# Banded attention and two FFNs on one core: the first FFN's eighth pair of weight chunks converted inline, and a smaller early allowance for the planner

## The chip, the core and the metric

The kernel runs on one core of a Trainium2 chip. The metric is the device time of one execution in microseconds. The core has five engines that run their own instruction streams in order: PE (TensorE, matmuls, with a separate row PEld for weight loads), DVE (VectorE), ACT (ScalarE), POOL (GpSimd) and SP (SyncE, which here only issues DMAs). They wait for one another through semaphores.

## The reference

```
attention: q, k, v of 4 x 8 heads x 576 tokens x 64
  scores = q k^T / 8, masked: heads 0-3 the last 32 keys, heads 4-7 every 4th of the last 128
  softmax over the keys, times v  ->  x: 2304 tokens x 512
first FFN:  h = x @ w_in (512 x 2048);  g = h if h > 0 else exp(h) - 1;  y = g @ w_out (2048 x 512)
second FFN: out = ((y @ w_a) * (y @ w_b)) @ w_out2        (512 x 1536, twice, then 1536 x 512)
```

The weights come to the chip as 64-bit floats. The kernel makes two 32-bit halves of each (a high part and a remainder), and each matrix product of the FFNs is three passes on TensorE: high x high, high x low, low x high.

## The kernel before

**Steps of the first FFN.** The tokens are cut in six blocks of 384 (t = 0 to 5), the 2048 hidden columns in 16 chunks of 128 (f = 0 to 15). One step s is one pair (t, f) of `STEPS1`: 7 steps of block 0, then all 16 of block 1 (steps 7 to 22), the remaining 9 of block 0 (23 to 31), then blocks 2 to 5, 96 steps in all. In a step PE does 12 matmuls into `ps_h` (line 525, "h(s)" below); ACT makes relu and exp of it into the tile `el` (lines 546 and 547), DVE joins them with line 552 ("el(s)" below), ACT and POOL split the result into the halves of `g` (lines 536 and 537), and two steps later PE does the 12 matmuls of the second product into four banks of `ps_y` (line 571, "y(s)" below). PE's order is h(s), y(s-2), h(s+1), y(s-1), and so on. There are two `ps_h` banks, so h(s+2) can start only when el(s) is done. When a block of tokens is complete its four `ps_y` banks are copied out, two by ACT (line 608) and two by DVE (line 606); for the first part of block 0 that is in step 8, and y(7) needs the same four banks again.

**Attention inside the steps.** Attention of block t+1 or so runs between the matmuls: scores (line 474), mask and maximum on DVE (490, 356), exp on ACT (360), normalisation on POOL (370), transposes (499) with ACT copies (502), values (514), and the split of x on ACT and DVE (462, 463). These tiles share two `ps_a` banks. For block 2 it starts at step 18, for block 3 at step 29.

**Weight conversion.** One chunk of w_in or w_out is 128 x 512 doubles. Converting it takes three ACT instructions (high word 252, low word 257, copy of the high part 278) and four on DVE (clamp 262, join 267, sign 270, remainder 297 or 854). Chunk f of w_out ("1o", f) and chunk f+2 of w_in ("1i", f+2) form a pair. There are two ways of doing it:

- inline: lines 1401 to 1404 put the two loads in step f-1 and the whole conversion (`w_convert`) in step f; the converted tile lies in the pool `pw`, named "w", which has 16 buffers, all used by the pairs f = 0 to 6 and the first two chunks;
- by the planner: `chunk_ops` splits the conversion into single operations, and `tick`, called twice a step from step 7 on (lines 1461 to 1464), places as many of them as the allowance of each engine admits. The allowance grows by `ROOM1` per tick in the first 32 ticks (steps 7 to 22) and by `ROOM` after that, and is spent by the costs in `COST` (0.7 for a 512-wide DVE operation, 0.67 on ACT). The converted tile lies in the pool "wb", which is opened in step 6. After the chunks of the first FFN the same list goes on with the weights of the second FFN (lines 901 and 917 are its DVE operations), whose results go to DRAM and come back later.

Both kinds share four buffers for raw weights (`wraw`) and four for the work tile (`wt`).

Of the kernel before, what the change touches and what calls it, by code (L numbers as in the profile page):

```python
# [36 lines left out]
SPLIT = 7  # L37
# [16 lines left out]
C1, C0, AHEAD, LAG_IN, LAG_OUT = SPLIT, NF1 + SPLIT, 56, 3, 2  # L54
LATE, LAG_LATE = 2 * (NF1 * (NB - 1) - C1), 7

ROOM1 = {"V": 1.8, "A": 1.4, "G": 0.9}
ROOM = {"V": 1.15, "A": 0.95, "G": 0.75}

FILL = [1, 1, 0, 1, 2, 1, 0] + [1, 1, 0, 1, 2, 0, 0]  # L60
# [2 lines left out]
ON0, ON1 = "AAV", "AAV"  # L63
# [152 lines left out]
def banded_attention_two_ffn(ctx: ExitStack, tc: tile.TileContext, ins, out):  # L216
    nc = tc.nc
    V, A, G, T, SP = nc.vector, nc.scalar, nc.gpsimd, nc.tensor, nc.sync
# [577 lines left out]
    def tick(behind_exp=False):  # L796
        now[0] += 1
        size = ROOM1 if now[0] <= 2 * (C0 - C1) else ROOM
        for e in room:
# [43 lines left out]
    def chunk_ops(key):  # L843

        at = {}
        x = assembly(at)(key)

        def hi():
            at["to"] = pools["wb"].tile([128, 2, 512], F32R, tag="w", name="w")
            part_hi("A", at["to"][:, 0, :], at["t", key])  # L850

        def lo():
            w = w_sb[key] = at["to"]
            V.tensor_tensor(w[:, 1, :], at["t", key], f32(w[:, 0, :]), op=SUB)

        give("wraw", x)
        give("wt", Op("V", 512, lo, Op("A", 512, hi, x)))
# [464 lines left out]
    def at_step(step, slot, fn, *args):  # L1322
        todo.setdefault((step, slot), []).append((fn, args))
# [70 lines left out]
    for f in range(NF1):  # L1394
        st = f
        ks = [("1o", f)] + ([("1i", f + 2)] if f + 2 < NF1 else [])
        if f >= SPLIT:
            for k in ks[::-1]:
                chunk_ops(k)
            continue  # L1400
        for k in ks:
            if k != ("1o", 0):
                at_step(max(0, st - 1), "B" if f else "L", w_load, k)
        at_step(st, "C", w_convert, ks, "w", ON1)


    def held(fn, *args):
# [170 lines left out]
```

## Time and profile before

| | us |
|---|---|
| median of 3 runs (lowest, highest) | 916.47 (914.46, 916.89) |
| the profiled execution | 915.85 |
| its span | 914.0 |
| PE busy in the span | 897.7 (98%) |
| DVE busy | 657.5 (72%) |
| ACT busy | 522.7 (57%) |
| POOL busy | 284.1 (31%) |

The span begins with the first instruction and ends with the last; the 1.85 us around it belong to the execution's time. The busy shares are means over very different stages: PE's row of tenths in the page reads 9 nearly everywhere, DVE's is between 8 and 9 in the first fifth and 5 to 7 after that.

### The profile page before, as it was taken

What the parts mean: (1) busy time and instruction counts of PE and PEld (TensorE: products, weight loads), DVE (VectorE), ACT (ScalarE), POOL (GpSimd) and SP (SyncE); (2) the same over time, 40 slices, a digit from 0 to 9 for tenths busy, and PEclk for the clock granted to TensorE, in tenths of its full rate; (3) what the DMA queues carried; (4) which work ended last, traced back from release to release, by engine and by line L of the source; (5) the groups of instructions that cost most, each with busy time, mean ns of one, the idle gap of its engine ahead of it and who ended that gap; (6) DMA issues with size and microseconds to landing.
All of it is one profiled execution on the core that took longest, in us unless ns stands there. A gap on an engine that the chain in (4) does not pass through costs nothing.

```text
span 914.0 us, 17034 instructions
## 1 busy us (share of the span) xinstructions
PE 897.7 (98%) x6157; PEld 862.7 (94%) x6157; DVE 657.5 (72%) x1147; ACT 522.7 (57%) x1328; POOL 284.1 (31%) x260
## 2 busy tenths in 40 slices
PE   9999999999999999999999999999999999999998
PEld 6789988899999999999999999999999999999998
DVE  6898899759767777767876366688746688656666
ACT  6898788777777777876766343325443225343231
POOL 2323234333333333332323122222622222522233
PEclk9999999999999999999999999999999999999999
DMA  9764344648656455645997588675787754687722
GB/s 286 227 225 164 134 150 144 219 144 271 198 178 217 157 176 192 207 160 184 327 356 270 179 289 281 226 259 179 233 329 252 252 196 144 226 311 242 243 69 70
DMA packets 75860, 195.80 MB, mean 214 GB/s; under 512 B 8288, under 2 KB 22240, under 8 KB 75776
## 3 DMA queue, kind: packets, MB, share of 16 engines
q1 hardware_dynamic: 63680, 175.70, 57.0%
q10 hardware_dynamic: 12096, 19.01, 5.7%
q8 instruction: 49, 0.80, 0.3%
q14 instruction: 35, 0.29, 0.1%
HBM read 151.16 MB, written 43.52 MB: 213 GB/s over the span
## 4 chain that ended last, share of the span: by engine, by line
PE 72%; DVE 4%; issue 1%; ACT 0%; DVEq 0%
PE ps_h L974 27%; PE ps_y L571 14%; PE ps_h L525 14%; PE ps_o L1290 13%; PE ps_s L474 1%; PE ps_v L514 1%; PE ps_o L1150 1%; PE ps_t L499 1%; DVE u L1082 0%; DVE yt L733 0%; DVE acc L1313 0%; DVE u L1064 0%; DVE y L703 0%; DVE wraw L917 0%; DVE u L1046 0%
## 5 line engine op out<-in xcount | busy, mean ns | idle before, releaser
L974 PE MATMUL ps_h<-y,w 128*128 128x384 f32 x1512 | 293.0, 337 | 1.5 <-DVE el L1029 1.1
L974 PEld LDWEIGHTS ps_h<-y,w 128*128 128x128 f32 x1512 | 256.0, 188 | 4.4 <-DVE el L1029 2.0
L571 PE MATMUL ps_y<-g,w 128*128 128x384 f32 x1152 | 224.4, 341 | 2.0 <-ACT w L278 1.4
L525 PE MATMUL ps_h<-x,w 128*128 128x384 f32 x1152 | 222.9, 340 | 3.6 <-DVE el L552 2.1
L525 PEld LDWEIGHTS ps_h<-x,w 128*128 128x128 f32 x1152 | 199.0, 188 | 9.0 <-DVE el L552 3.2
L571 PEld LDWEIGHTS ps_y<-g,w 128*128 128x128 f32 x1152 | 200.4, 189 | 6.3 <-ACT w L278 1.8
L537 POOL TENSOR_TENSOR g<-el,g 128x384 fp32r<-128x384 f32 x96 | 116.6, 1215 | 276.7 <-ACT g L536 230.7
L1290 PE MATMUL ps_o<-w,g 128*128 128x256 f32 x1071 | 153.4, 281 | 0.4 <-ACT g L1090 0.4
L1290 PEld LDWEIGHTS ps_o<-w,g 128*128 128x128 f32 x1071 | 147.2, 188 | 0.9 <-ACT g L1090 0.9
L552 DVE SCALAR_TENSOR_TENSOR el<-el,ps_h 128x384 f32<-128x384 f32 x96 | 53.0, 552 | 80.4 <-ACT el L547 78.0
L1016 POOL TENSOR_TENSOR g<-el,g 128x384 fp32r<-128x384 f32 x34 | 38.4, 1131 | 121.7 <-ACT g L1015 106.8
L1313 DVE TENSOR_TENSOR acc<-acc,ps_o 128x512 f32<-128x512 f32 (+1 forms) x77 | 49.7, 645 | 34.3 <-PE ps_o L1290 34.0
L546 ACT ACTIVATE el<-ps_h 128x384 f32<-128x384 f32 x96 | 46.5, 485 | 38.4 <-PE ps_h L525 33.6
L267 DVE SCALAR_TENSOR_TENSOR wt<-wt,wraw 128x512 uint32<-128x512 uint32 x68 | 62.2, 919 | 3.8 <-ACT wraw L257 1.4
L270 DVE SCALAR_TENSOR_TENSOR wt<-wraw,wt 128x512 uint32<-128x512 uint32 x68 | 60.5, 895 | 0.8
L536 ACT ACTIVATE g<-el 128x384 fp32r<-128x384 f32 x96 | 49.6, 516 | 16.7 <-DVE el L552 16.6
L370 POOL TENSOR_TENSOR e<-e,rs 96x512 f32<-96x512 f32 (+2 forms) x40 | 40.7, 1018 | 47.1 <-DVE rs L369 47.1
L547 ACT ACTIVATE el<-el 128x384 f32<-128x384 f32 x96 | 50.2, 523 | 1.7
L360 ACT ACTIVATE e<-e,nm 96x128 f32<-96x128 f32 x128 | 49.8, 391 | 0.7
L257 ACT ACTIVATE wraw<-wraw 128x512 uint32<-128x512 uint32 x68 | 45.1, 669 | 5.4 <-DMA wraw<-in_w2o 2.8
L1064 DVE TENSOR_TENSOR u<-ps_h,u 128x384 f32<-128x384 f32 x36 | 20.0, 557 | 39.0 <-PE ps_h L974 39.0
L1025 ACT COPY el<-ps_h 128x384 f32<-128x384 f32 x36 | 17.2, 478 | 50.4 <-PE ps_h L974 50.4
(111 smaller groups left out, 1084.0 us busy)
## 6 DMA issues: line engine op xcount, KB each, us to landing
w<-w2P_o SPq DMA_DIRECT2D x52, 512.0 KB, 5.6
w<-w2P_a SPq DMA_DIRECT2D x48, 512.0 KB, 4.5
w<-w2P_b SPq DMA_DIRECT2D x48, 512.0 KB, 4.4
wraw<-in_w1i SPq DMA_DIRECT2D x16, 512.0 KB, 4.1
wraw<-in_w1o SPq DMA_DIRECT2D x16, 512.0 KB, 3.5
wraw<-in_w2a SPq DMA_DIRECT2D x12, 512.0 KB, 3.6
wraw<-in_w2b SPq DMA_DIRECT2D x12, 512.0 KB, 3.6
wraw<-in_w2o SPq DMA_DIRECT2D x12, 512.0 KB, 3.8
```

Source lines behind the costliest of these rows:

```text
L267: V.scalar_tensor_tensor(t, t, 3, L, op0=ALU.logical_shift_left, op1=ALU.bitwise_or)
L270: V.scalar_tensor_tensor(t, H, 0x80000000, t, op0=ALU.bitwise_and, op1=ALU.bitwise_or)
L360: A.activation(e[:, i], sc[:, i], AF.Exp, bias=nm[:, i : i + 1], scale=scale, accum_out=sm[:, i : i + 1],)
L525: T.matmul(ps[:, :TB], w[:, wi, kc * 128 : (kc + 1) * 128], xs[kc][:, xi, :], start=(n == 0), stop=(n == 3 * KC - 1),)
L536: A.activation(g[:, 0, :], gf, AF.Copy)
L537: G.tensor_tensor(g[:, 1, :], gf, f32(g[:, 0, :]), op=ALU.subtract)
L547: last_e[0] = A.activation(e, e, AF.Exp, scale=-1.0)
L552: last_g[0] = V.scalar_tensor_tensor(e, e, -1.0, h_ps.pop(s)[:, :TB], op0=ALU.add, op1=ALU.max)
L571: T.matmul(y_ps[t][c][:, :TB], w[:, wi, c * 128 : (c + 1) * 128], g[:, gi, :], start=(first and n == 0), stop=(last and n == 2),)
L974: last_mm[0] = T.matmul(ps[:, :TB], w[:, wi, kc * 128 : (kc + 1) * 128], y2[S, yop][kc][:, xi, :], start=(start and n == 0), stop=(n == 5) ...
L1290: T.matmul(ps[:, 256 * n : 256 * n + 256], g[name][:, gi, i * 128 : (i + 1) * 128], w[:, wi, h, :], start=((first or not held) and n == m ...
L1313: V.tensor_tensor(a, a, ps[:, :n], op=ADD)
```

## The change

The pair f = 7 (chunk 7 of w_out and chunk 9 of w_in) is converted inline in step 7 instead of by the planner, into buffers of "wb". The planner is left with 14 chunks of the first FFN instead of 16, and its allowance per tick in steps 7 to 22 goes from 1.8 to 1.5 on DVE and from 1.4 to 1.2 on ACT.

```diff
-ROOM1 = {"V": 1.8, "A": 1.4, "G": 0.9}
+ROOM1 = {"V": 1.5, "A": 1.2, "G": 0.9}
 ...
     for f in range(NF1):
         st = f
         ks = [("1o", f)] + ([("1i", f + 2)] if f + 2 < NF1 else [])
-        if f >= SPLIT:
+        if f > SPLIT:
             for k in ks[::-1]:
                 chunk_ops(k)
             continue
         for k in ks:
             if k != ("1o", 0):
                 at_step(max(0, st - 1), "B" if f else "L", w_load, k)
-        at_step(st, "C", w_convert, ks, "w", ON1)
+        at_step(st, "C", w_convert, ks, "w" if f < SPLIT else "wb", ON1)
```

The loads of the new pair stand in SP's queue where the planner's first two loads stood; the planner's loads begin two places later. What moves on the engines is shown at three places. The first is DVE's stream in steps 6 to 9; lines 262, 267, 270 and 297 are conversion, 552 is el, 606 the copies out of `ps_y`. Before:

```order
125 L463 TENSOR_TENSOR x<-ps_v,x 128x4x96
126 L297 TENSOR_TENSOR w<-wt,w 128x512 x2
127 L552 SCALAR_TENSOR_TENSOR el<-el,ps_h 128x384
128 L606 COPY el<-ps_y 128x384
129 L552 SCALAR_TENSOR_TENSOR el<-el,ps_h 128x384
130 L606 COPY el<-ps_y 128x384
131 L552 SCALAR_TENSOR_TENSOR el<-el,ps_h 128x384
132 L262 TENSOR_SCALAR wt<-wt 128x512
```

And in the changed kernel:

```order
126 L297 TENSOR_TENSOR w<-wt,w 128x512
127 L262 TENSOR_SCALAR wt<-wt 128x512
128 L297 TENSOR_TENSOR w<-wt,w 128x512
129 L262 TENSOR_SCALAR wt<-wt 128x512
130 L267 SCALAR_TENSOR_TENSOR wt<-wt,wraw 128x512
131 L552 SCALAR_TENSOR_TENSOR el<-el,ps_h 128x384
132 L267 SCALAR_TENSOR_TENSOR wt<-wt,wraw 128x512
133 L270 SCALAR_TENSOR_TENSOR wt<-wraw,wt 128x512 x2
134 L552 SCALAR_TENSOR_TENSOR el<-el,ps_h 128x384
135 L297 TENSOR_TENSOR w<-wt,w 128x512 x2
136 L606 COPY el<-ps_y 128x384 x2
137 L552 SCALAR_TENSOR_TENSOR el<-el,ps_h 128x384
```

Eight conversion instructions came in around el(7) and el(8), and both copies of line 606 now stand behind the last two of them. On PE, y(7) is split there in the changed kernel: 3 matmuls, then 7 of h(10), then its other 9.

The second place is DVE's stream between el(16) and el(17), as an example of the steps that the planner fills; 854 is the planner's remainder. Before:

```order
175 L552 SCALAR_TENSOR_TENSOR el<-el,ps_h 128x384
176 L854 TENSOR_TENSOR w<-wt,w 128x512
177 L270 SCALAR_TENSOR_TENSOR wt<-wraw,wt 128x512
178 L262 TENSOR_SCALAR wt<-wt 128x512
179 L267 SCALAR_TENSOR_TENSOR wt<-wt,wraw 128x512
180 L270 SCALAR_TENSOR_TENSOR wt<-wraw,wt 128x512
181 L552 SCALAR_TENSOR_TENSOR el<-el,ps_h 128x384
```

In the changed kernel:

```order
175 L552 SCALAR_TENSOR_TENSOR el<-el,ps_h 128x384
176 L262 TENSOR_SCALAR wt<-wt 128x512
177 L854 TENSOR_TENSOR w<-wt,w 128x512
178 L267 SCALAR_TENSOR_TENSOR wt<-wt,wraw 128x512
179 L270 SCALAR_TENSOR_TENSOR wt<-wraw,wt 128x512
180 L552 SCALAR_TENSOR_TENSOR el<-el,ps_h 128x384
```

Four conversion instructions stand in the step instead of five. Counted in the two streams from the start of the kernel, the conversion instructions on DVE are 64 before and 72 now through step 8, 95 and 98 through step 14, 111 in both through step 17, 149 and 144 through step 25, 159 in both through step 29; from step 30 on the changed kernel is four to nine behind, and behind the last el of the first FFN stand 11 instead of 5.

The third place is ACT's stream in steps 10 and 11; 546 and 547 are relu and exp, 536 the high half of g, the others conversion. Before:

```order
138 L536 ACTIVATE g<-el 128x384
139 L278 ACTIVATE w<-wt 128x512
140 L257 ACTIVATE wraw<-wraw 128x512
141 L546 ACTIVATE el<-ps_h 128x384
142 L278 ACTIVATE w<-wt 128x512
143 L547 ACTIVATE el<-el 128x384
144 L257 ACTIVATE wraw<-wraw 128x512
145 L252 ACTIVATE wt<-wraw 128x512
```

In the changed kernel:

```order
142 L536 ACTIVATE g<-el 128x384
143 L252 ACTIVATE wt<-wraw 128x512
144 L546 ACTIVATE el<-ps_h 128x384
145 L547 ACTIVATE el<-el 128x384
146 L278 ACTIVATE w<-wt 128x512
147 L252 ACTIVATE wt<-wraw 128x512
```

The copy 278, which waits for DVE's line 270, stood between relu and exp of step 11 and now stands behind the exp.

## Rows read from the trace of the kernel before

**Rows 1.** Busy time by stretch: each engine's us (instructions), then PEclk, DMA share, GB/s.
```profile
78.48:109.69 31.21, 31.21 (x181) 31.21 (x181) 24.49 (x39) 24.45 (x50) 8.54 (x8) 1.00 0.44 149
109.69:168.87 59.18, 53.51 (x326) 49.27 (x325) 52.60 (x88) 46.20 (x126) 20.27 (x16) 0.97 0.48 164
162.00:166.00 4.00, 4.00 (x22) 3.72 (x23) 3.05 (x6) 1.42 (x4) 0.00 (x0) 0.57 1.03 331
...
240.00:420.00 180.00, 180.00 (x1242) 172.57 (x1241) 132.60 (x234) 137.83 (x396) 61.46 (x55) 1.00 0.54 181
...
505.00:545.00 40.00, 40.00 (x247) 39.35 (x247) 18.88 (x33) 15.65 (x33) 7.83 (x8) 1.00 0.74 237
```

**Rows 2.** What PE waited for, 112 to 170 us: total, times, longest.
```profile
PE ps_h L525 <- DVE el L552: 2.1, 4, 1.1
PE ps_s L474 <- DVE x L463: 1.6, 1, 1.6
PE ps_v L514 <- ACT pt L502: 1.4, 1, 1.4
PE ps_y L571 <- POOL g L537: 0.4, 1, 0.4
```

**Rows 3.** PE in order of time: start us, us, line, count, [idle before, releaser].
```profile
86.81 2.24 PE L571 MATMUL ps_y<-g,w 128*128 128x384 f32 x12
...
107.61 2.25 PE L571 MATMUL ps_y<-g,w 128*128 128x384 f32 x12
109.69 2.25 PE L525 MATMUL ps_h<-x,w 128*128 128x384 f32 x12
...
135.05 2.35 PE L525 MATMUL ps_h<-x,w 128*128 128x384 f32 x12 [1.06 <-DVE el L552]
...
163.52 3.43 PE L571 MATMUL ps_y<-g,w 128*128 128x384 f32 x12
...
168.87 2.24 PE L571 MATMUL ps_y<-g,w 128*128 128x384 f32 x12
...
173.72 0.68 PE L571 MATMUL ps_y<-g,w 128*128 128x384 f32 x3
174.34 1.12 PE L474 MATMUL ps_s<-qk 64*96 64x128 f32 x16
...
177.15 0.88 PE L514 MATMUL ps_v<-pt,v 128*64 128x96 f32 x16
...
182.23 0.83 PE L499 MATMUL ps_t<-ident,e 96*128 96x96 f32 x8
...
306.50 0.49 PE L499 MATMUL ps_t<-ident,e 96*128 96x96 f32 x4
```

**Rows 4.** DVE in order of time.
```profile
79.29 0.55 DVE L552 SCALAR_TENSOR_TENSOR el<-el,ps_h 128x384 f32<-128x384 f32 x1 [0.66 <-ACT el L547]
79.80 0.56 DVE L606 COPY el<-ps_y 128x384 f32<-128x384 f32 x1
...
85.34 0.69 DVE L267 SCALAR_TENSOR_TENSOR wt<-wt,wraw 128x512 uint32<-128x512 uint32 x1
...
86.89 1.51 DVE L267 SCALAR_TENSOR_TENSOR wt<-wt,wraw 128x512 uint32<-128x512 uint32 x1
...
89.04 0.55 DVE L552 SCALAR_TENSOR_TENSOR el<-el,ps_h 128x384 f32<-128x384 f32 x1
...
113.81 0.55 DVE L552 SCALAR_TENSOR_TENSOR el<-el,ps_h 128x384 f32<-128x384 f32 x1 [1.33 <-ACT el L547]
...
308.12 0.55 DVE L552 SCALAR_TENSOR_TENSOR el<-el,ps_h 128x384 f32<-128x384 f32 x1 [0.53 <-ACT el L547]
```

**Rows 5.** ACT in order of time.
```profile
76.12 0.63 ACT L278 ACTIVATE w<-wt 128x512 fp32r<-128x512 f32 x1 [2.36 <-DVE wt L270]
...
98.15 0.63 ACT L278 ACTIVATE w<-wt 128x512 fp32r<-128x512 f32 x1 [1.99 <-DVE wt L270]
...
165.61 0.69 ACT L257 ACTIVATE wraw<-wraw 128x512 uint32<-128x512 uint32 x1 [2.55 <-DMA wraw<-in_w2o]
```

**Rows 6.** POOL in order of time.
```profile
86.39 1.46 POOL L537 TENSOR_TENSOR g<-el,g 128x384 fp32r<-128x384 f32 x1 [3.27 <-ACT g L536]
```

## The prediction

> **What bounds the kernel now.** I read the page first: PE is busy 98% of the span, so only the places where PE waits, or runs slowly after a wait, can give time back. The view of busy time by stretch shows where those lie. In the 180 us from 240 to 420 PE is busy for all 180, and in the 31.21 us from 78.48 to 109.69 for all 31.21; in the 59.18 us from 109.69 to 168.87 it is busy 53.51, at a mean granted clock of 0.97 [rows 1]. The view of waits says for what: el four times (2.1 us), x of line 463 (1.6), the copy pt of line 502 (1.4), g (0.4) [rows 2]. The reader is to see that all of these are made on DVE and ACT. In that stretch DVE is busy 52.60 of 59.18 us, in the one before only 24.49 of 31.21 [rows 1].
>
> The timeline shows how it comes to that. el(s) may end as late as 3 groups of 12 matmuls after h(s), since h(s+2) starts there. A group takes 2.08 us: ten of them lie between the starts at 86.81 and 107.61 [rows 3]. So the limit is 6.24 us. h(10) ends at 86.81 and el(10) starts at 89.04, 2.23 us later; h(15) ends at 107.61 and el(15) starts at 113.81, 6.20 later [rows 3, 4]. In five steps the planner's five DVE instructions a step have used up the whole reserve, with ACT and DVE waiting for each other on the way: line 278 waited 1.99 us for line 270 at 98.15 and held up the exp behind it [rows 5]. All that attention adds from step 18 on then falls on PE.
>
> **What that stretch loses.** From 109.69 to 168.87 the timeline has 21 groups, three sets of scores, one of transposes and one of values. The 21 groups are 43.7 us. A set of scores inside y costs 3.43 (173.72 to 177.15) less 2.08 = 1.35; three are 4.05. From 168.87 to 182.23 are 13.36 us with 5 groups, one set each of transposes, scores and values: 13.36 - 10.40 - 1.35 = 1.61 for transposes and values [rows 3]. Together 49.4; the stretch took 59.18, so it loses 9.8. Part of that is the clock: from 162 to 166 the granted clock is 0.57, most of it at the lower level of 1.2 GHz, after the waits of 1.4 and 1.6 us, and the y at 163.52 shows 3.43 us [rows 1 to 3].
>
> **The change part by part.** *The planner's share of steps 15 to 25.* By the counts in the two streams, DVE does 149 - 95 = 54 conversion instructions there before and 144 - 98 = 46 now. At 52.60 us for 88 instructions, 0.60 each [rows 1], that takes off 4.8 and leaves 47.8 busy. If DVE idles as much in between as now (59.18 - 52.60 = 6.6), the stretch cannot be shorter than 54.4 by DVE alone. But now it would be entered with the reserve unspent: four conversions a step plus el are 5 x 0.60 = 3.0 us and one POOL hold of 0.8 (below) against 4.16 for two groups, so the lag should stay near the 2.23 of el(10), 4.0 us below the limit. 54.4 - 4.0 = 50.4. The ends are 49.4 (nothing lost) and 54.4 (no reserve). I take 51.4: 50.4 plus 1.0 that I leave to the waits for pt and x, which hang on ACT copies standing behind el in line and not on el alone. Gain 7.8, between 4.8 and 9.8. The clock's part comes back with the waits.
>
> *The pair in step 7.* On ACT six instructions are added; ACT stood idle 2.36 us before the 278 at 76.12 [rows 5], and the first two fit there if the load has landed, which it should, since it takes the place in SP's queue of a load that is already issued at that time. If not, relu of step 7 is late, and what follows is the same wait as next. On DVE the three instructions ahead of el(7) take up to 1.8, of which 0.66 was idle [rows 4]: el(7) starts at 79.29 + 1.1 = 80.4 and ends at 80.9. Behind it, up to the end of the first copy of line 606, lie five conversions (3.0), el(8) and the copy (0.56 each): 85.0. Before, that copy started at 79.80 [rows 4]. y(7) is due two groups before 86.81, at 82.65; in its new split the bank of that copy is asked for after 3 + 7 matmuls, at 84.4. So PE waits 0.6 there. What waits behind it is all of PE; the second copy comes 0.5 later and is asked for 1.0 later.
>
> *What POOL does to that.* The L267 at 86.89 took 1.51 us beside the POOL subtract of 86.39 to 87.85, the one at 85.34 took 0.69 [rows 4, 6]: 0.8 more. Two such subtracts, of steps 7 and 8, fall among the added instructions. The Trainium skill (SBUF — State Buffer, Who interferes with whom) says that a VectorE instruction with two inputs in SBUF and a GpSimd instruction that reads SBUF exclude each other, the one that starts second waiting for the whole of the first; by that rule 267, 270 and 297 of the pair are each exposed and the wait would be 0.6 + 2 x 0.8 = 2.2, without it 0.6; the trace agrees in the row above. Only holds that fall on the chain to the copy count, and the copy itself reads PSUM. Bounds 0 and 2.2; I take 0.9, nearer to 0.6 because of the waits for ACT in which a hold can hide.
>
> *Later.* From step 30 on the planner's work is four to nine DVE instructions behind. Nothing asks for it soon: PE has no wait from 240 to 420 [rows 1]. At the end six more instructions (3.6 us) run behind the last el, where DVE is busy 18.88 of 40 us [rows 1]; I cost them at nothing, at most one in front of a PSUM read, 0.6. DMA moves the same bytes.
>
> **The sum.** 7.8 - 0.9 = 6.9. Against the profiled execution: 915.85 - 6.9 = 908.95. The median of the runs is 0.62 above that execution, so 909.6.
>
> **Rivals.** *The load comes back with attention.* Only the waits for el and g (2.5 us) [rows 2] go. Those for pt and x stay, and the clock falls again, because steps 26 to 29 now hold 15 conversion instructions instead of 10 beside attention. For it: the counts are equal again at step 29, so the same work ends at the same step, and 47.8 busy of 51.4 is 93%. Against it: DVE's idle time before 109.69, 6.7 of 31.21 us, is used now, and those late steps had no waiting PE. Time: 916.47 - 2.5 + 0.9 = 914.9.
>
> *Slower: ACT caught at a raw chunk that hasn't landed.* In the changed stream line 257 stands in each four-step cycle of steps 36 to 76 ahead of the softmax and the relu of the step in which its load may still be under way; at 165.61 such a 257 waited 2.55 us [rows 5]. At h(s) ending 306.50 and el(s) starting 308.12 the lag is 1.62 [rows 3, 4], so 4.6 are free; two more conversions in that step (1.2) and a wait like that one (2.55) use 3.75. It decides only if the loads come 0.9 later still. Then each of 11 cycles costs what goes beyond; at 1.0 each 909.6 + 11 = 920.6. Against it: that margin stands in every cycle, and the place of the load is only shifted by a step.
>
> **How the numbers follow.** The forecast has 0.70, with its own range from 907 (nothing lost in the stretch, 916.47 - 9.8 + 0.3) to 914.6 (gain 4.8 less 2.2 and 0.6, so 2.0). The attention rival has 0.20, the slower one 0.10. The range from 907.0 to 915.0 leaves out the slower one and half of what lies at the edges. 0.3% is 2.75 us, about what runs of this kernel can tell from no change: below 913.7 is faster, above 919.2 slower. Of the forecast 0.68 lies below 913.7 and 0.02 between; of the attention rival 0.05 below and 0.14 between, 0.01 above; of the slower rival 0.09 above and 0.01 between. Faster 0.73, same 0.17, slower 0.10.
>
> **What would show it.** Right: in the profile after, PE's waits for el between 110 and 150 us are gone, el starts 2 to 4 us after its h in steps 10 to 17, the waits for pt and x are under 1 us together, no half clock near 163, and one new wait of y(7) for line 606 near 84. The whole shift stands by 170 us: from there to the end the two traces run at the same pace. Wrong: waits for el that reappear in steps 20 to 30, a wait at y(7) above 2 us, or waits of PE anywhere from 170 to 500.

## The result, and the profile after

The changed kernel takes 922.40 us (median of 7 runs, 919.02 to 924.25); the kernel before took 916.89 beside it (7 runs, 914.46 to 920.04). The ratio is 1.0053 with a 95% interval of 1.0032 to 1.0073: slower by 5.5 us, outside the forecast range. The profiled execution took 922.40 with a span of 920.6 (before 914.0).

The page's first part, part 4 (shares of the chain that ended last) and the group of line 257:

```profile
PE 899.7 (98%) x6155; PEld 864.8 (94%) x6157; DVE 649.2 (71%) x1147; ACT 523.4 (57%) x1328; POOL 283.0 (31%) x260
...
PE 62%; DVE 12%; ACT 8%; DMA 7%; issue 2%; ACTq 0%; SPq 0%; DVEq 0%
...
L257 ACT ACTIVATE wraw<-wraw 128x512 uint32<-128x512 uint32 x68 | 45.5, 674 | 34.4 <-DMA wraw<-in_w2b 10.8
```

PE is as busy as before, 98%, but ACT now stood idle 34.4 us ahead of line 257 (5.4 before). The chain that ended last was 72% PE, 4% DVE, 0% ACT and had no DMA before; now 12% of it are DVE, 8% ACT, 7% DMA and 62% PE. The stretches of [rows 1], after:

```profile
78.48:109.69 31.21, 31.05 (x177) 30.39 (x176) 30.32 (x45) 26.27 (x53) 10.31 (x8) 1.00 0.52 183
109.69:168.87 59.18, 55.41 (x349) 53.00 (x347) 47.15 (x79) 45.26 (x129) 19.20 (x16) 0.97 0.42 147
162.00:166.00 4.00, 4.00 (x19) 4.00 (x18) 3.96 (x7) 2.52 (x11) 1.31 (x1) 0.71 0.96 356
240.00:420.00 180.00, 179.16 (x1233) 171.09 (x1232) 125.25 (x230) 135.67 (x392) 58.03 (x54) 1.00 0.54 182
```

DVE's work did move forward: 24.49 to 30.32 us in the first stretch, 52.60 to 47.15 in the second. PE gained 1.9 us of busy time in the second. But the granted clock still falls there (0.71 from 162 to 166 us, 0.57 before), and from 240 to 420, where PE had no wait, it now has one. PE's waits, first for 112 to 170 us (answer to [rows 2]), then for 466 to 505 us, where before had none:

```profile
PE ps_s L474 <- DVE x L463: 3.2, 1, 3.2
PE ps_y L571 <- POOL g L537: 0.5, 1, 0.5
```

```profile
PE ps_h L525 <- DVE el L552: 2.7, 1, 2.7
```

The waits for el and pt are gone; that for x has doubled; one of 2.7 us has come at the end. PE at four places in order of time (answer to [rows 3]); the third, a second wait for x at 221 us, and the fourth, at the end of block 3, are the two longest between 170 and 466 us:

```profile
82.95 1.06 PE L571 MATMUL ps_y<-g,w 128*128 128x384 f32 x3
83.84 1.40 PE L525 MATMUL ps_h<-x,w 128*128 128x384 f32 x7
85.08 2.08 PE L571 MATMUL ps_y<-g,w 128*128 128x384 f32 x9
...
159.58 1.11 PE L474 MATMUL ps_s<-qk 64*96 64x128 f32 x14 [3.22 <-DVE x L463]
160.62 3.91 PE L571 MATMUL ps_y<-g,w 128*128 128x384 f32 x12
...
221.36 1.11 PE L474 MATMUL ps_s<-qk 64*96 64x128 f32 x14 [1.28 <-DVE x L463]
...
371.58 1.33 PE L571 MATMUL ps_y<-g,w 128*128 128x384 f32 x6 [0.84 <-ACT el L608]
```

Where the time went is read best from the starts of h(s) on PE, run against run. The table gives them for every kernel of this study, as us behind (+) or ahead (-) of the kernel before, one profiled execution each; the last column is the span's difference. h(27) lies behind the x wait of step 25.

| kernel | h(11) | h(25) | h(27) | h(36) | h(68) | h(84) | h(95) | span |
|---|---|---|---|---|---|---|---|---|
| before, absolute | 88.89 | 157.61 | 171.56 | 219.58 | 377.73 | 452.24 | 498.00 | 914.0 |
| changed kernel | +1.07 | -3.98 | -2.41 | -2.26 | +0.21 | +0.50 | +5.79 | +6.6 |
| e1 inline pair only | +1.99 | -1.44 | +1.06 | +2.12 | +10.38 | +12.60 | +14.79 | +14.7 |
| e2 allowance only | +0.91 | +1.74 | -1.93 | -0.41 | +6.26 | +7.66 | +12.38 | +13.9 |
| e3 caught up | +1.05 | -3.69 | -1.71 | -1.66 | +2.99 | +2.99 | +3.50 | +3.7 |
| e4 before, two ticks held | -0.13 | -0.11 | -0.11 | +3.89 | +8.92 | +9.52 | +14.44 | +14.7 |
| e5 new front, old rest | +0.94 | -4.15 | -2.51 | -1.72 | -1.68 | -1.68 | -0.55 | -0.7 |
| e6 the same from step 24 | +0.35 | -4.03 | -4.67 | -3.59 | -3.60 | -3.60 | -2.58 | -2.7 |
| e7 old front, new rest | +2.45 | +2.63 | -0.68 | -0.51 | +6.23 | +6.41 | +10.78 | +11.0 |
| e8 pair only, old order | +1.14 | +0.76 | +0.73 | +0.74 | +0.77 | +0.76 | +0.77 | +0.8 |
| e9 light step 25 | +1.25 | -3.78 | -2.81 | -2.15 | -2.70 | -2.70 | -2.69 | -2.5 |
| e10 old order at the end | +1.97 | -2.58 | +0.16 | +0.27 | +5.24 | +9.25 | +9.25 | +9.5 |
| e11 fetches put off | +0.86 | -4.30 | -1.35 | -1.19 | +3.91 | +4.59 | +7.90 | +8.9 |
| e12 behind the exp | +2.87 | -1.52 | +0.03 | +0.09 | +5.13 | +5.88 | +7.64 | +7.9 |
| e13 one step late | +0.47 | +0.53 | +0.50 | +0.50 | +3.64 | +4.65 | +6.22 | +7.3 |
| e14 four steps late | +0.63 | +0.71 | +0.71 | +0.72 | +0.73 | +0.72 | +3.63 | +5.0 |
| e15 light steps 24, 25 | +1.60 | -3.18 | -5.79 | -1.19 | -1.74 | -1.74 | -0.80 | -0.8 |

The changed kernel is 4 us ahead at h(25), keeps 2.3 after the x wait, loses 2.8 from h(36) to h(84), and 5.3 from there to h(95). Kernels whose streams are the same up to some step still differ there between executions (e4, e7, e13 and e14 are the kernel before up to step 23, and stand between -0.1 and +2.6 at h(25)): a single column is read to that. The size of a loss along a row varies too: the changed kernel, e7, e11 and e12 have the same instructions on DVE, ACT and PE in the steps from 32 to 84 and lose 2.8, 6.9, 5.8 and 5.8 from h(36) to h(84). What is plain is that they lose, since e5, e6 and e8, with the old order there, lose 0.04 at most. The medians decide on totals.

### The profile page after: what moved, and what is told of

The parts are those of the page before. It is cut to its first block, busy times and chain, and to the rows that moved or that the text cites. A ratio compares the mean times of both kernels' runs of the same rounds, so it can differ in the third digit from the quotient of the medians.

```text
span 920.6 us, 16977 instructions
## 1 busy us (share of the span) xinstructions
PE 899.7 (98%) x6155; PEld 864.8 (94%) x6157; DVE 649.2 (71%) x1147; ACT 523.4 (57%) x1328; POOL 283.0 (31%) x260
## 4 chain that ended last, share of the span: by engine, by line
PE 62%; DVE 12%; ACT 8%; DMA 7%; issue 2%; ACTq 0%; SPq 0%; DVEq 0%
PE ps_h L974 26%; PE ps_o L1290 13%; PE ps_y L571 10%; PE ps_h L525 10%; ACT e L360 2%; DMA wraw<-in_w2b 1%; DMA w2P_a<-wraw 1%; ACT el L547 1%; DVE wt L267 1%; DVE el L552 1%; DVE wraw L901 1%; DVE wt L270 1%; DMA w2P_b<-wraw 1%; PE ps_o L1150 1%; DMA wraw<-in_w2o 1%
## 5 line engine op out<-in xcount | busy, mean ns | idle before, releaser
L257 ACT ACTIVATE wraw<-wraw 128x512 uint32<-128x512 uint32 x68 | 45.5, 674 | 34.4 <-DMA wraw<-in_w2b 10.8
L267 DVE SCALAR_TENSOR_TENSOR wt<-wt,wraw 128x512 uint32<-128x512 uint32 x68 | 54.8, 809 | 2.3 <-ACT wraw L257 1.1
L252 ACT ACTIVATE wt<-wraw 128x512 f32<-128x512 f32 x68 | 45.1, 666 | 12.4 <-DMA wraw<-in_w2b 3.4
L270 DVE SCALAR_TENSOR_TENSOR wt<-wraw,wt 128x512 uint32<-128x512 uint32 x68 | 51.2, 759 | 0.4
```

The costliest lines, as they stand in the source:

```text
L267: V.scalar_tensor_tensor(t, t, 3, L, op0=ALU.logical_shift_left, op1=ALU.bitwise_or)
L270: V.scalar_tensor_tensor(t, H, 0x80000000, t, op0=ALU.bitwise_and, op1=ALU.bitwise_or)
```

## The experiments

The first theory was **lateness**: the planner, four to seven DVE instructions behind from step 31 on, loads the last raw chunks too late. Four runs.

**e1, the inline pair with the old allowance** (`ROOM1` back to 1.8 and 1.4).

> The pair of step 7 inline, the planner's allowance left at 1.8 and 1.4. By DVE's stream the planner is then three to five conversion instructions ahead of the kernel before from step 30 on, where the changed kernel is seven behind. Theory (the loss of the changed kernel is made by the planner's lateness in steps 85 to 95, the inline pair itself costs only 0.8 us at y(7) and wins 2 to 3 us back by step 25): no wait of PE over 1 us and no half clock near 480 us, time 911 to 915. Rival (the inline pair costs by itself, whatever the planner does): 919 to 923 as the changed kernel. Second rival (the weight traffic of the second FFN is at its limit near 480 us in any case and an earlier planner does not help): the stall near 480 us stays, 917 to 920.

Measured 931.56 us (ratio 1.0157, 1.0142 to 1.0171). A planner that is ahead loses 14.5 us: PE waits 5.3 of them, in two waits, for the copies of line 608, at the ends of blocks of tokens. Lateness can't be the whole cause.

**e2, the new allowance without the pair** (the diff's first hunk alone).

> The smaller allowance alone, the eighth pair left to the planner. By DVE's stream the planner is then eleven to thirteen conversion instructions behind the kernel before, twice as late as in the changed kernel. Theory (lateness makes the loss at the end): the early waits for el between 110 and 150 us are shorter than before by 1 to 2 us, and the last ten steps lose 6 us or more against the kernel before, time 920 to 926. Rival (the inline pair is what costs): 912 to 917, with no stall near 480 us.

Measured 929.05 (1.0128, 1.0114 to 1.0141): beyond the theory's range. The loss is again spread from h(36) to the end.

**e3, the changed kernel caught up:**
```diff
+ROOM2, TICKS2 = {"V": 1.8, "A": 1.4, "G": 0.9}, range(33, 53)
         size = ROOM1 if now[0] <= 2 * (C0 - C1) else ROOM
+        size = ROOM2 if now[0] in TICKS2 else size
```


> The changed kernel with an allowance of 1.8 and 1.4 per tick in ticks 33 to 52 (steps 23 to 32) instead of 1.15 and 0.95. By DVE's stream the planner has caught up by step 26 and is three conversion instructions ahead of the kernel before from then on. Steps 7 to 22 are those of the changed kernel. Theory (lateness): as the changed kernel up to step 24, 4 us ahead of the kernel before; the wait for x near 160 us as in the changed kernel or longer, since steps 23 to 26 hold more conversion; no stall at 480 us; time 912 to 917. Rival (the inline pair, or the smaller allowance in steps 7 to 22, costs by itself at the end): 919 to 923.

Measured 921.83 (1.0048, 1.0034 to 1.0063). The stall near 480 us is gone, as the theory said, and the time is hardly better: 4.7 us go between h(36) and h(68), 1.8 each at h(51) and h(67): these are block ends, and both copies of line 608 stand behind a 252 and a 257 on ACT there.

**e4, the kernel before with two ticks passed over:**
```diff
         now[0] += 1
+        if now[0] in range(48, 50):
+            return
```


> The kernel before with two of the planner's ticks passed over (ticks 48 and 49, in step 30). Up to step 30 the streams are those of the kernel before; from step 31 the planner's place is that of the changed kernel to the instruction (seven DVE conversion instructions behind, five in steps 88 to 93). Theory (lateness alone makes the loss): nothing lost up to step 31, then the same small losses after step 37 as in the changed kernel (about 1 us at step 37, 1 us at steps 67 to 71) and the stall at h(90) with the half clock behind it, 4 to 6 us together with the end: 920 to 924. Rival (the loss needs what the inline pair or the allowance changed ahead of step 30): 915 to 918, no stall at 480 us.

Measured 929.69 (1.0138, 1.0124 to 1.0152). The hole itself cost 4 us by h(33), which was not foreseen, and the streams equal the changed kernel's from step 42 only. From h(36) on it loses 5.6 to h(84) and 4.9 to h(95): the stall at h(90) is there (2.97 us) with nothing of the change in the kernel.

All four point at where the planner's operations stand after step 30. To move that alone, the planner's order was written out and replayed:

```diff
+FROM_TICK = 46
+ORDER = [...]   # for each tick, the operations that the kernel before placed in it
...
+        if now[0] >= FROM_TICK and now[0] <= len(ORDER):
+            done = ORDER[: now[0]] if now[0] == FROM_TICK else ORDER[now[0] - 1 : now[0]]
+            due.extend(i for row in done for i in row if every[i].at is None)
...
+                x = every[due.pop(0)]   # instead of the first operation that is ready
```

**e5, the changed kernel to step 29, then the old order** (`FROM_TICK = 46`).

> The changed kernel through step 29; from step 30 on the planner places each single operation in the tick in which the kernel before placed it (its order is written out as a table, and what is still missing is caught up in step 30). Theory A (it is the planner's order after step 30, which the change shifted by four to seven DVE instructions, that costs; the first 30 steps win): 2.2 us ahead of the kernel before at h(30), nothing lost after that, no stall at 480 us: 913.5 to 916. Rival B (the first 30 steps of the changed kernel leave something behind, as later loads or a later clock, that costs whatever the planner does then): 919 to 923.

Measured 915.65 (0.9985, 0.9973 to 0.9998).

**e6, the same from step 24 on** (`FROM_TICK = 34`).

> As the run that goes over at step 30, but the order of the kernel before holds from step 24 on, so that four DVE conversion instructions more stand in steps 24 and 25, ahead of the join of x that PE waits for at 160 us. Theory A: 3 us ahead of the kernel before at h(24); the wait for x of line 463 stays 2 to 3 us with a half clock behind it; from step 30 on nothing lost: 913.5 to 917. Rival B: 919 to 923.

Measured 915.28 (0.9981, 0.9967 to 0.9995).

**e7, the other cross** (the kernel before, with the changed kernel's order as `ORDER`, from tick 34).

> The other cross: the kernel before through step 23, its eighth pair left to the planner; from step 24 on each planner operation stands in the tick in which the changed kernel placed it. Theory A: the same time as the kernel before up to step 24, then the waits of the changed kernel: for el of line 608 at h(67), for el of line 552 at h(90) with the half clock, together 7 to 9 us between steps 30 and 95: 922 to 926. Rival B (the cost lies in what the first 24 steps changed): 915 to 918.

Measured 924.17 (1.0074, 1.0052 to 1.0096).

**e8, the pair inline, everything else in its old tick** (the changed kernel, `FROM_TICK = 1`).

> The inline pair alone: every other planner operation stands in the tick in which the kernel before placed it, so that the planner has only fewer operations in steps 7 to 11 and the streams of DVE and ACT are those of the kernel before from step 12 on. Theory A: 0.8 us lost at y(7) behind the two copies of line 606, given back by the waits for el at 110 to 135 us, which are entered with the same lag as in the kernel before only if the lag has run full by then; from step 24 on as the kernel before: 915.5 to 918. Rival B (the inline pair costs by itself): 919 to 923.

Measured 916.75 (0.9997, 0.9984 to 1.0010).

All four times lie in theory A's ranges. With the change of order at step 24, the new order of the rest costs 7.1 us behind the new front (922.40 against 915.28, e6) and 7.4 behind the old (924.17 against 916.76); the new front wins 1.5 and 1.8. The pair alone costs nothing that the median shows. In the table e5, e6 and e8 run flat from h(36) to h(84). Three details missed: in e6 the expected wait for x and its half clock were not there (no wait for x from 112 to 170 us, granted clock 1.00 from 158 to 168), e5 and e6 still lose 1.1 and 1.0 after h(84), and e7's profiled execution lost 11 us after h(36), not 7 to 9.

**e10, the changed kernel with the old order for the last steps** (its own order to tick 138, then at most two 512-wide DVE operations a tick until the old order is reached).

> The changed kernel up to step 75; from there the planner catches up, two 512-wide DVE operations a tick at most, and has the order of the kernel before from step 83 on. Theory A (the two ticks by which the changed order is late in the last steps put the last loads and line 257 where the data has not landed): the small losses of steps 25 to 71 stay (about 1.2 at step 37 and 1.1 at step 67), the wait of 2.7 us at h(90) and its half clock are gone: 5 us less than the changed kernel, 916 to 918.5. Rival C (the stall at h(90) comes from the weight traffic near 480 us whatever the planner's place): 920 to 924.

Measured 925.77 (1.0096, 1.0082 to 1.0110). The time missed both ranges. The stall at h(90) went as theory A said: from h(84) to h(95) nothing is lost (changed kernel 5.3). But the catching up fell on a block end and cost 2.8 at h(83), PE waiting 1.69 us for line 608, and this execution had lost 5.0 from h(36) to h(68), where the changed kernel's lost 2.5.

**e11, no fetches in steps 84 to 91:**
```diff
-        w2_fetch_next(s - 1, 1)
+        if not 84 <= s < 92:
+            w2_fetch_next(s - 1, 1)
```


> The changed kernel with no fetch of converted weights of the second FFN started in steps 84 to 91; they are fetched after that, so that the second FFN may wait for them and the time of the whole tells little. Read at h(90). If the full DMA engines make the load of the last raw chunk late (rival C, or theory A with the traffic as a partner): DMA share in 440 to 480 us well under 0.98, line 257 waits less than 1 us, no wait at h(90). If the load is late only because its buffer comes free late (theory A without the traffic): the wait of 2 to 3 us at h(90) stays.

Measured 924.86 (1.0086, 1.0072 to 1.0100). The share of busy DMA stayed at 0.96 and 0.97 in 440 to 480 us, so the run doesn't meet its own condition. But the wait at h(90) is nearly gone, with line 257 in the same place between relu and exp:

```profile
483.00 0.67 ACT L257 ACTIVATE wraw<-wraw 128x512 uint32<-128x512 uint32 x1 [1.65 <-DMA wraw<-in_w2o]
```

It waits 1.65 us here and 3.28 in the changed kernel, and PE then 0.33 against 2.73. The store that frees the buffer took 3.96 us, where it took 6.8, 6.2, 6.3 and 6.4 in the changed kernel, e7, e4 and e12; the load 4.07 against 5.36 (but 4.06 in e12). That points at the fetches as a part of the stall; one execution, already 4.1 us later at h(84) and with a wait of 0.99 us for g ahead of h(85), doesn't show how large a part.

**e12, ACT's planner instructions behind the exp:**
```diff
+                late = behind_exp or now[0] >= 160
-                after = last_e if behind_exp and x.eng == "A" else last_g
+                after = last_e if late and x.eng == "A" else last_g
```


> The changed kernel, but from step 87 on all of the planner's ACT instructions stand behind the exp of their step, where before half of them could be moved ahead of it. In step 88 line 257 then stands behind the exp and ahead of the high half of g. Theory A: h(90) no longer waits for el; y(88) may wait up to 1.5 us for g instead; 3 to 5 us less than the changed kernel, 917 to 920. Rival D (line 257 is only where the wait shows, el would be late without it too): h(90) waits 2 to 3 us as in the changed kernel, 921 to 924.

Measured 922.26 (1.0047, 1.0029 to 1.0066). The wait at h(90) is gone and h(84) to h(95) loses 1.8 instead of 5.3. The load landed late here too, at 483.94 us, and the exp of step 88 had started at 479.78: line 257 ahead of the exp was what made el late. The rest is a wait of 1.1 us at h(92), where another ACT copy stands ahead of the exp. The median lies in rival D's range and shows no gain on the changed kernel's 922.40; the profiled execution had lost 5.4 more by h(84). So the trace decides here, not the total.

**e13 and e14, the kernel before, shifted late by one step and by one whole cycle of the attention** (its own `ORDER` from tick 1, with two or eight empty ticks put in at tick 67).

> The kernel before with its planner order written out and nothing placed in ticks 67 and 68 (step 40 to 41); everything after stands two ticks, one step, later. Lateness theory and place theory both: from step 44 on the planner's 252, 257 and 278 stand in the steps of the softmax; losses of about 1 us at the block ends, h(51) and h(67), some 3 to 7 us from step 44 to 84, and a wait of 2 to 3 us with a half clock near h(90): 921 to 927.

> The kernel before with nothing placed in ticks 67 to 74; everything after stands eight ticks, four steps, later, which is one whole cycle of the attention, so that between steps 47 and 79 the streams have the planner's instructions in the same places of the cycle as before, one pair of chunks later. Place theory: nothing lost from step 47 to 84 (h(84) within 0.5 us of the kernel before); the end is not told by it, since the attention has stopped there and the weights come four steps later to the second FFN: 917 to 924. Lateness theory: at least as much lost between steps 44 and 84 as in the run that is one step late (3 us or more), 924 or more.

Measured 923.21 (1.0078, 1.0058 to 1.0098) for one step and 921.46 (1.0059, 1.0037 to 1.0081) for four. Four steps late loses 0.00 us from h(36) to h(84); one step late loses 4.15, about half a microsecond in every cycle. PE's waits from 190 to 420 us are an empty list in both; the 1 us at the block ends that was expected of e13 is not there, and its wait near h(90) is 1.3 us instead of 2 to 3. The price of one step is in PE's own order; one cycle of e13 and then of the kernel before (names of lines differ, 702 and 514 are the values, 713 and 525 h, 759 and 571 y):

```profile
274.71 0.38 PE L702 MATMUL ps_v<-pt,v 128*64 128x96 f32 x2
275.02 0.44 PE L713 MATMUL ps_h<-x,w 128*128 128x384 f32 x1
275.39 0.88 PE L702 MATMUL ps_v<-pt,v 128*64 128x96 f32 x14
276.20 2.17 PE L713 MATMUL ps_h<-x,w 128*128 128x384 f32 x11
278.21 2.25 PE L759 MATMUL ps_y<-g,w 128*128 128x384 f32 x12
```

```profile
274.19 0.88 PE L514 MATMUL ps_v<-pt,v 128*64 128x96 f32 x16
275.00 2.35 PE L525 MATMUL ps_h<-x,w 128*128 128x384 f32 x12
277.19 2.25 PE L571 MATMUL ps_y<-g,w 128*128 128x384 f32 x12
```

From values to y it is 3.50 us against 3.00: the stream's builder, with the planner's instructions elsewhere, split the values around one matmul of h, and PE is busy for all of it; the last copy of pt had ended at 274.09. All eight sets of values from 274 to 417 us are split in e13, at the block ends around more matmuls, and none in the kernel before, in e14 and in the changed kernel, which pays by waits instead. Place in the cycle decides in the middle of the kernel, lateness does not. At the end e14 loses 2.9; attention has stopped there, so the shift changes place and lateness together, and this run can't tell them apart.

**e9 and e15, meant to beat both.** e9 is the changed kernel through the first half of step 24, with nothing placed to the end of step 25, then at most 2.5 operations of 512 a tick until the old order is reached; e15 starts the pause half a step earlier.

> A version meant to beat both: the changed kernel through step 23, no planner operation placed in steps 24 (second half) to 25, so that on DVE the copies of line 606 and the join of x stand next to each other in step 25; then at most 2.5 operations of 512 a tick until the order of the kernel before is reached (step 35), which holds to the end. Theory A: no wait for x at 160 us and no half clock after it, 5 to 6 us ahead of the kernel before at h(26), of which the fuller steps 27 to 31 take back up to 2: 911.5 to 914. Rival E (what is put off comes back as waits for el in steps 27 to 31): 915 to 918.

> As the version with a light step 25, but the planner places nothing in the first half of step 24 either, so that ACT's copy 278 of 256 columns, which waits 1.0 us for line 917 there, no longer stands ahead of relu(24). If that copy made relu, el and then x late: the wait for x at 160 us falls from 2.5 to 1.2 us or less and the half clock after it goes; 1 to 3 us less than that version, 911.5 to 914. If what is put off costs as much in steps 26 to 35: 914 to 917.

Measured 914.51 for e9 (0.9973, 0.9961 to 0.9984) and 913.85 for e15 (0.9971, 0.9960 to 0.9982), 2.6 and 3.2 us under the kernel before. In e9 the wait for x stayed at 2.5 us, against theory A. The reason is ACT, here of the changed kernel, with DVE's half of x behind it:

```profile
153.77 0.42 ACT L278 ACTIVATE wt<-wt 128x256 fp32r<-128x256 f32 x1 [0.99 <-DVE wraw L917]
...
154.59 0.49 ACT L546 ACTIVATE el<-ps_h 128x384 f32<-128x384 f32 x1 [0.40 <-ACT wt L278]
...
157.76 0.49 ACT L462 ACTIVATE x<-ps_v 128x384 fp32r<-128x384 f32 x1 [0.40 <-ACT el L608]
```

```profile
158.98 0.55 DVE L463 TENSOR_TENSOR x<-ps_v,x 128x384 fp32r<-128x384 f32 x1
```

The planner's copy waits for DVE and holds relu(24); exp, g, both copies 608 and the ACT half of x queue behind it, and only then comes DVE's half, in the changed kernel behind two planner instructions more (262 and 267). e9 has the copy still, at 153.97 with 1.00 of waiting. In e15 neither the copy nor anything else of the planner is in that half step. PE's waits of e15 from 112 to 170 us:

```profile
PE ps_y L757 <- POOL g L723: 0.7, 1, 0.7
PE ps_s L660 <- DVE x L649: 0.6, 1, 0.6
```

x costs 0.6 there, no half clock follows (granted clock 1.00 from 158 to 168 us), and h(27) is 5.8 us ahead. Then 4.6 of that go back in steps 27 to 33, where what was put off is caught up beside the attention of block 3.

## Why the prediction was wrong, step by step

The profiled execution took 13.5 us more than the sum gave for it (922.40 against 908.95). By the table, 4.5 of them are missing by h(27) (2.4 us ahead instead of 6.9), 8.2 are lost from there to h(95), 0.8 after that.

**The place of the loss at y(7): right, its cause by half.** The changed kernel goes from +0.27 at h(9) to +1.07 at h(11), 0.8 us against 0.9. PE's list of waits shows nothing of it; the list of the weight loads, from 78 to 92 us, does:

```profile
PEld ps_y L571 <- POOL g L537: 0.4, 1, 0.4
PEld ps_y L571 <- DVE el L606: 0.4, 1, 0.4
```

Half is the forecast wait for line 606, half one for POOL's part of g, which the prediction did not have. DVE and then POOL after (answers to [rows 4] and [rows 6]):

```profile
78.56 0.69 DVE L297 TENSOR_TENSOR w<-wt,w 128x512 fp32r<-128x512 f32 x1
...
82.83 2.48 DVE L297 TENSOR_TENSOR w<-wt,w 128x512 fp32r<-128x512 f32 x2
85.23 1.01 DVE L606 COPY el<-ps_y 128x384 f32<-128x384 f32 x2
...
110.03 0.55 DVE L552 SCALAR_TENSOR_TENSOR el<-el,ps_h 128x384 f32<-128x384 f32 x1 [0.35 <-ACT el L547]
```

```profile
81.34 2.00 POOL L537 TENSOR_TENSOR g<-el,g 128x384 fp32r<-128x384 f32 x1 [6.14 <-PE ps_y L571]
83.61 1.15 POOL L537 TENSOR_TENSOR g<-el,g 128x384 fp32r<-128x384 f32 x1 [0.28 <-ACT g L536]
```

Two 297, one of which takes 0.69 us where POOL is still (at 78.56 us), took 2.48 beside both subtracts. POOL's first subtract took 2.00 beside the conversions (its second 1.15), and y(7) waited for it. That is what the Trainium skill (SBUF — State Buffer, Who interferes with whom) says of two engines that exclude each other. The prediction counted only what POOL costs DVE.

**The reserve of el: right.** el(15), 6.20 us behind its h in [rows 3, 4], is 1.35 behind here (110.03 less 108.68), and the four waits for el are gone. From h(11) to h(25) the kernel gains 5.05 us.

**The gain of 7.8: too large by 4.3, at the term of 1.0 left for pt and x.** From h(11) to h(27) the gain is 3.48 (+1.07 to -2.41). The prediction put the waits for pt and x under 1 us together because they hang on copies behind el; pt went, x rose from 1.65 to 3.22 and the y behind it took 3.91 us (3.43 in [rows 3]) at the lower clock (granted 0.50, which is 1.2 GHz, from 162 to 164 us). What x hung on was a planner copy ahead of relu(24), which the changed order put there. The 7.8 were there to be had for a while: e15 goes from +1.60 to -5.79, 7.4, and gives 4.6 back by h(33). (The upper edge of the forecast's own range, 914.6, is 914.5 by its own terms; nothing hangs on it.)

**"Later": the step that failed.** "Nothing asks for it soon: PE has no wait from 240 to 420" took an empty list of waits for a reserve. The list was empty because the old order fits the attention's cycle (e14 against e13). In the new order the planner's work falls ahead of copies that PE waits for. The first place is h(37). ACT and then DVE of the changed kernel:

```profile
219.26 0.66 ACT L252 ACTIVATE wt<-wraw 128x512 f32<-128x512 f32 x1 [1.98 <-DMA wraw<-in_w2b]
...
220.24 0.48 ACT L462 ACTIVATE x<-ps_v 128x384 fp32r<-128x384 f32 x1
```

```profile
220.75 0.56 DVE L463 TENSOR_TENSOR x<-ps_v,x 128x384 fp32r<-128x384 f32 x1 [1.81 <-ACT x L462]
```

The planner's 252 waits for a raw chunk; g and ACT's half of x stand behind it, DVE's half behind that, and PE waits 1.28 (the 221.36 above). h(37) is 1.2 us later by it; e7, e10, e11 and e12 lose 0.9 to 1.4 there, e5, e6 and e8 nothing. The second place is the end of block 3; ACT of the changed kernel, then of the kernel before:

```profile
364.97 0.20 ACT L358 ACTIVATE nm<-nm 96x4 f32<-96x4 f32 x1 [1.23 <-DVE nm L356]
...
366.77 0.62 ACT L278 ACTIVATE wraw<-wraw 128x512 fp32r<-128x512 f32 x1
...
367.39 0.47 ACT L546 ACTIVATE el<-ps_h 128x384 f32<-128x384 f32 x1
...
371.06 0.47 ACT L608 COPY el<-ps_y 128x384 f32<-128x384 f32 x1
```

```profile
364.03 0.20 ACT L358 ACTIVATE nm<-nm 96x4 f32<-96x4 f32 x1 [1.02 <-DVE nm L356]
...
365.82 0.47 ACT L546 ACTIVATE el<-ps_h 128x384 f32<-128x384 f32 x1
...
369.59 0.47 ACT L608 COPY el<-ps_y 128x384 f32<-128x384 f32 x1
```

The kernel before has no conversion on ACT between 363 and 371 us; its second copy starts 1.47 us earlier, although PE comes there 0.92 us later. About 0.9 of this comes from DVE, whose maximum (line 356) starts at 364.27 behind a 270 and a 917 of the planner, against 363.32 behind a 901; about 0.5 from the 278 on ACT ahead of relu. In the changed kernel PE waits 0.84 (the 371.58 above). In this execution h(37) and this block end make 2.3 of the 2.8 us from h(36) to h(84); e7, e11 and e12, in the same order, lose 5.8 to 6.9 there, and why executions differ is open.

**The slower rival: the right instruction, the wrong bill.** It had line 257 caught at a raw chunk that hasn't landed, at 1.0 us in each of 11 cycles, and 0.10. Line 257 does wait; ACT's waits from 190 to 420 us after (before and e14 have none of these):

```profile
ACT wraw L257 <- DMA wraw<-in_w2a: 7.5, 6, 2.3
ACT wraw L257 <- DMA wraw<-in_w2b: 6.3, 4, 2.2
ACT wraw L257 <- DMA wraw<-in_w2o: 6.2, 6, 2.3
```

That is 20 us on ACT, and nearly all of it is hidden, as the prediction argued for every cycle. PE's waits in those 230 us are 2.1, the two above, and one of them is the rival's mechanism with line 252 in the place of 257: at h(37) ACT is caught at a raw chunk. It shows once more, at the end, where the load's buffer is freed by a store and the share of busy DMA is 0.98 (460 to 480 us). The chain of waits into h(90):

```profile
466.98 6.76 DMA w2P_a<-wraw
...
473.81 5.36 DMA wraw<-in_w2o
...
479.20 0.65 ACT wraw L257
479.85 0.42 ACT el L547
...
480.36 0.56 DVE el L552
...
480.97 1.35 PE ps_h L525 x5
```

Store, load, 257, exp, el, h: line 257 stands between relu (475.45) and exp (479.75) and keeps the exp 3.28 us. PE waits 2.73, and the granted clock is then 0.91 from 480 to 500 us, with 0.50 from 482 to 484; together 4.6 by h(91). The loads of that unit were issued at 467.95 and 470.18 before and at 473.81 and 480.21 after. Shown: line 257's place ahead of the exp makes el late (e12); the shifted order brings the stall without the change's front (e4, e7), and the old order has none (e5, e6, e10). Not separated: how much the fetches have in the slow store and load, though e11 points at them.

**The other rival**, attention taking the load back, foresaw the x wait and the half clock that stayed, but not what the new order costs after step 36.

## What to carry to other kernels

An empty list of waits says that the order fits, not that there is room: before moving work "that nothing asks for", look at what will stand behind it on each in-order engine at the rare places (block ends, the last loads), and price one step's shift there. When a heuristic is changed at one point, fix the order everywhere else (replay it) before judging the change: here the same edit was 5.5 us slower with the heuristic left to itself and 1.1 to 1.5 us faster with the old order held behind it (e5, e6). And shift a schedule by a step and by a whole cycle: for as long as the cycle runs, the first tells the price of place and the second that of lateness.

## What the runs showed that was not expected

- A shift of eight ticks, a whole cycle, cost 0.00 us over 48 steps (e14), a shift of two ticks 4.15 (e13), in one profiled execution each.
- PE loses 0.50 us where one matmul of h is placed inside a set of values, without idling: no list of waits shows it.
- Two 512-wide DVE subtracts of two SBUF inputs took 2.48 us beside two subtracts of POOL, where one alone takes 0.69.
- ACT's line 257 waited 20 us for raw loads in 190 to 420 us; PE's waits there were 2.1 in all, traced to other instructions of the planner.
